# A reloaded weight block moved to dead key storage, and a new hand-written order for a sparse attention and gated feed-forward kernel

## The chip, the cores and the metric

The kernel runs on one core of one Trainium2 chip. The core has five engines that run side by side, each with its own queue of instructions, worked off in order: TensorE (PE, with its weight loads as a row of their own, PEld), VectorE (DVE), ScalarE (ACT), GpSimd (POOL) and SyncE (SP). Semaphores make one engine wait for another or for a transfer. The metric is the device time of the one launch in microseconds.

## What is computed

Block-sparse attention over 4 batches, 8 heads, 768 positions and a head size of 64, then a gated feed-forward layer over the 3072 tokens. The reference, cut to what matters:

```python
scores = scale * np.matmul(q, k.transpose(0, 1, 3, 2))
mask = (np.abs(blk_i - blk_j) <= 1) | first and last block row and column
for qb in range(n_blocks):
    for kb in sampled_blocks[qb]:
        mask[block qb, block kb] = True
attn = softmax(np.where(mask, scores, -1e9))
x = (attn @ v) as tokens x 512
gate = 1.0 / (1.0 + np.exp(-(x @ w_gate)))      # 512 x 1536
return (gate * (x @ w_val)) @ w_out             # 1536 x 512
```

## The kernel before, in words

The work is cut into 12 units, numbered 0 to 11: four batches of three blocks of 256 query rows. Each unit has four pairs of heads, p = 0 to 3. Everything is float16 on the way into TensorE.

For a unit n and a pair p, three steps j make scores (a task `s{n}.{p}.{j}.qk` on PE), each followed by the exponential on ACT (`.exp`, line 597, 128x1024 values). When the three are done, one product with the 0/1 mask on DVE follows (`s{n}.{p}.3.mask`, line 624, 128x3072 float16 values, both operands and the result in SBUF). Then PE multiplies with the values in two halves (`pv{n}.{p}.a` and `.b`), DVE normalizes (`nrm`), and a transposing DMA on SP's queue (`xc`) turns the result.

The feed-forward layer follows in groups g of one or two units. A task `f{g}.{j}` has two halves on PE, then a tanh on ACT (`.th`, line 823) and a gating product on DVE (`.ga`, line 826). The product with `w_out` is done for five pairs of units as a seven-product scheme (`z1` to `z5`: products `A`, `B`, `P3`, `P4`, `P5` on PE; sums of operands `S1` to `S4` on DVE, line 962; results `p1`, `u2`, `c11`, `u3`, `c22`, `c12`, `c21` on DVE, line 1027, or as a plain scaled copy on ACT, line 1101, or DVE, line 1103). Units 0 and 11 go without it (`y0`, and `y11` in the method `y_last`). The scheme needs four differences of blocks of `w_out`; one of them, `T3`, is written over the block `wo[:, 0:HF, UQ:2*UQ]` of `w_out` itself (HF is 6, UQ is 256). So `y_last`, which needs that block once more, gets it by a second load from HBM, the task `ldw0` (line 1086).

Batches 1 to 3 are loaded one batch ahead, for each pair p, by three tasks on GpSimd's queue (line 220): `ldk{b}.{p}`, `ldq{b}.{p}`, `ldv{b}.{p}`, 192 KB each, into `k16`, `q16` and `v16`. For k and q a copy follows into a ring of four buffers `pr` (`kup{b}.{p}`, `qup{b}.{p}`), and a transposing DMA on SP's queue (`kxb`, `qxb`, line 545) into `kT` or `qT`. For v a copy into `vex` follows (`vc{b}.{p}`). These copies are short and any of three engines may make them: POOL (line 279), ACT (line 277) or DVE (line 281). After the copies of batch 3 nothing reads `k16` again.

Nothing in the kernel decides the order while it runs. All 1066 tasks are listed first (`plan.add`), and the string `ORDER` says in which order they are emitted: a number is a task; a letter behind it (A, D, G) chooses another engine than the task's first; `:2` is the PSUM bank (four of them) that a task takes; `@457` makes a load wait until the PE task 457 is done. `j3` is filler work on PE. Each engine gets its tasks in the order in which they stand in this string, and works them off in that order. A load on POOL that waits at its gate holds everything that stands behind it on POOL.

The tasks of which the prediction speaks, by number: 457 is `s5.0.2.qk`, 539 `s6.0.1.qk`, 374 `ldk2.2`, 414 `ldk2.3`, 271 `kup2.0`, 383 `s4.1.0.qk`; 168 and 116 are `ldv1.1` and `ldv1.0`, 220, 181, 257 and 262 `vc1.1`, `vc1.0`, `vc1.2` and `vc1.3`, 365 and 327 the mask products `s3.3.3.mask` and `s3.2.3.mask`, 234 and 228 the gatings `f1.5.ga` and `f1.3.ga`, 300 and 367 `pv3.0.a` and `pv3.2.a`; 245 is `ldq1.3`, 260 and 258 `qup1.3` and `kup1.3`, 261 and 259 their transposes, 328 `s3.3.0.qk`; 556 is `s6.1.1.qk`, 287 `ldv2.0`, 302 `vc2.0`, 560 `s6.1.3.mask`, 562 `pv6.0.a`; 518, 519, 520 and 521 are `z2.c11`, `z2.u3`, `z2.c22` and `z2.P3.a`.

Of the kernel before, what the change touches and what calls it, by code (L numbers as in the profile page):

```python
# [19 lines left out]
B, H, S, D = 4, 8, 768, 64  # L20
# [19 lines left out]
FFN_LAG = 3  # L40
VW = 80
ORDER = """
j3 j3 j3 j3 j3 j3 j3 j3 6 17 14 11A 7:0 18:3 8 15:2 19A 16 9:1 23:0 38:3 39 40:2 24 10 21:0 41 86:1
26:3 87A 82:2 22 27 42:0 46:1 43 47 83 12:3 31:2 13 32 33:0 34 36:3 37 84:2 28:0 62:1 63 85 50:2 51
29 70:0 96@70 20 88:3 44:1 30 71 89 52:2 72:3 90:0 45 73 56:1 91 53 74:3 4@56 0@56 3@56 25 149@56 75
60:2 66:0 80:3 81 57 61 54:1 92:2 48:3 67 111:0 93 112 55 113:1 114 225@113 49 64:3 35 97:2 76:0 65
125@113 98 106:3 77 107 68:1 78:2 69 121:0 79 99:1 122 58:3 100 59 144:2 145 165:1 123:3 124 115
130:0 131 126:2 132 133 147:3 146 166 148 103:0 127 138:1 128 104 134:3 2@103 139 129 109:1 110
1@103 94:0 163:2 135 95 136 179:1 180 164 137 153:0 105 182:1 5@182 154 251:2 252 150:3 183 193:2
151 194 155 167 240:0 241 156:1 152 157 117:2 201 108@240 184:3 191 185 118 187:0 192 158 249:2 202  # L50
169:1 223:3 188 250 140:0 170 224 141 205:2 189:0 171 198@205 206 161G 190 243:3 244 199:0 200 195
172 159:2 258 160A 221:0 173 162 203:3 101:2 186@203 102 245@203 142G 143 238G 222 174 204 218:0 177
196:2 175D 197 259 253 276:3 219 277 207 212:1 282:2 213 214 260A 242 247G 283 209:3 210 211 215:1
261 265:2 216 235 217 266 239 168@265 236 237 273:3 255:1 263:2 274 264 256 119:0 268 120 284:3 269
270 248 285 116@284 328:0 275 329 279 246 229:2 230 231 286 363:1 220G 361:3 362 364 232:0 208@361
325:2 233 326 305:3 226:1 181 234 254@305 300:0 287@305 303:2 306 365 278@303 257G 330@303 227 228
262G 301 304 320 446@303 389:3 449G 390 321 327 322 292:1 380:2 381 293 294 295 331 367:3 410:2 358
178 368 375 432:0 411 280G 370:1 433 376 377 371 296:2 372:0 373 297 267@372 332 366@372 298 333 386
299 383:3 384 288:1 391:0 392 289 316:2 290 302G 435:3 317 382 312:0 437@435 291 412:1 385@412 436
318 681@412 307@412 393 319 323G 313 176 413 314 315 407:3 441:1 442 408 460:2 427 308:0 461 434  # L60
443:1 428 309 444 463:2 399:1 429 438 450:3 310 311 464 335 336 447:0 530:2 281 451 400 445 448
338:3 531 401 402 337 414@530 457:2 324 339 374@457 454 458 341 532:1 533 342 347:2 271G 359A 369
455 272 343 589@532 387G 456 452:1 340 482:0 334 344 348 346 349 453 353:1 459 483 345 539:0 504:3
350 540 430G 505 354 465:0 466 351 484:3 355 378G 395:1 501:0 485 352 480:2 388 467 396 537:3
597@537 481 502 561@537 498 360 397 538 462 398 564G 419:0 503 547:1 548 499 500 558:3 559 420 421
472:1 379 575:2 439 576 422 565:3 473 535:0 566 403:2 536 529 567:3 440 474 534 431 475 404 550:1
542 568 490:3 405 406 394@550 409G 617@550 551 543 544 593:2 491 549 594 492 493 556:1 415:0 553
578:2 557 560 416 579 417 418 423:1 586:3 587 562:2 424 563 425 584:3 585 476:0 426 570 614:1 615
603:3 577 604 571 572 477 468:1 588 581 606:2 478 479 590:3 607 469 591 470 471 598 595:2 596
552@595 599 600 658:0 486:1 605 612:2 696G 554G 633:3 487 632G 659 660@633 613 634 494:0 630:2 495  # L70
488 496 616 489 655:3 497 631 650 506 357 656 592 609 618:1 651 652 676:0 677 507 619 620 356 638:3
580@676 678:0 541@678 639 733:2 679 621 509:1 608@733 640 641 734 747:0 748 742:3 508 510 512D 518:2
582G 583 743 513 511 635:0 727:3 636 569@727 519 514 728 735:0 736 697:3 698 515 516 657 517 626:0
520 740:3 627 730:1 741 628 521 680 694:3 731 629 545G 546 601G 522 695 699:1 674A 700 673 523 755:0
724 555 524:2 725 756 737 767:1 602 768 525 726 622:0 526 753:3 573 574 754 729 661:1 623 624 610
625 646:2 662 663 738:3 750:0 751 647 739 664 648 770:1 744 669:0 649 760:2 771 637@760 527 761 745
762:1 763 670 749 746 671 672 642:2 682:1 643 644 773:3 774 758:0 683 757 759 645 764 848:3 684
665:2 765 752 685 849 686:1 675 666 667 766 769 775:0 668 687 690:3 776 611 688 790:0 653G 654 831:2
691 791 832 777 808 689 811:2 692 693 701 702 772 732 812 778:1 829:3 830 809 850:2 779 851 780 810
782:3 893:2 894 781 704:0 814:1 792:2 793 528 705 703 707D 708 783 815 784 794:2 800:1 795 709 878:2  # L80
# [5 lines left out]
962:0 963 856 864:2 854 926:1 858D 859 921:0 927 922 865 860 920 943:1 945:0 903 944 857 946 861 863  # L86
# [4 lines left out]
1029 1038 1049 1005 1006:0 1031:2 1007 1032 1033 1050 1030 1015:3 1009D 1010 1039:1 1011 1040 1041  # L91
1012 1034 1016 1042 1014 1021:2 1043:1 1008 1017 1022 1018 1023 1025 1044 1026 1019 1045 1013D 1020
1051:2 1052 1046 1053 1054 1056:0 1057 1058 1061:3 1062 1063 1024 1059 1055 1064 1065 1060
# [58 lines left out]
def kernel(  # L152
# [153 lines left out]
    def both(bank):  # L306
        return units_ps[bank.slot]
# [28 lines left out]
    def tiled(out, lhsT, rhs, start, stop):  # L336
        return nc.tensor.matmul(out, lhsT, rhs, start=start, stop=stop, skip_group_check=True).ins  # L337
# [441 lines left out]
    class Ffn:  # L779
# [168 lines left out]
        def z(self, mate):  # L948
# [129 lines left out]

            stored[0] = [plan.add(key + "st0", [(SP, 0.45)], store(0, b, u), [c11, c12], dma=("O", 0))]
            stored[1] = [plan.add(key + "st1", [(SP, 0.45)], store(1, b2, u2), [c21, c22], dma=("O", 0))]  # L1080
            if self.z_ == last_z:
                back.append(
                    plan.add(
                        "ldw0",
                        [(DMA, 0.72)],
                        lambda eng: nc.gpsimd.dma_start(  # L1086
                            wo[:, 0:HF, UQ : 2 * UQ],
                            moe_w_out.rearrange("(f p) m -> p f m", p=128)[:, 0:HF, UQ : 2 * UQ],
                        ),
                        [pb, t3],  # L1090
                        dma=("L", 0.393),
                    )
                )
# [86 lines left out]
    def later(b):  # L1180
# [155 lines left out]
```

## Time and profile before

| | us |
|---|---|
| median of 3 runs | 284.26 |
| lowest and highest of them | 282.92, 290.8 |
| the profiled execution's own time | 282.64 |
| its span, first to last instruction | 280.9 |
| PE busy within the span | 270.7 |
| DVE, ACT, POOL busy within the span | 210.6, 187.7, 76.9 |

Times within the profile count from the first instruction. A row of a view of groups gives line, engine, operation, what is written and read, how often, the sum of busy time and the mean of one in ns, then the engine's idle time ahead of it and what ended that. A row of the timeline gives start and duration in us, and in brackets the engine's idle time ahead and what ended it. The table by stretches gives busy time of each engine, the granted clock of TensorE as a share, the share of the DMA engines and GB/s.

### The profile page before, as it was taken

To read this page: it belongs to the slowest core of one execution; us is meant where nothing else is said; L and a number is where in the kernel's file an instruction comes from. 1 tells how busy PE (TensorE), PEld (TensorE's weight loads), DVE (VectorE), ACT (ScalarE), POOL (GpSimd) and SP (SyncE) were. 2 spreads that over 40 slices of the span, in tenths; PEclk is the share of its full clock that TensorE was granted. 3 is DMA by queue.
4 is the path that set the end of the run, shared out by engine and by line. 5 is a ranking of instruction groups with operands and counts; after the bars stand their busy time and mean duration, and the time that the engine had idled before them with its cause. 6 is when DMAs were issued, how large, how long until landed. Compare 5 with 4: busy or idle time off the path is not lost.

```text
span 280.9 us, 11919 instructions
## 1 busy us (share of the span) xinstructions
PE 270.7 (96%) x5459; PEld 208.6 (74%) x5459; DVE 210.6 (75%) x282; ACT 187.7 (67%) x231; POOL 76.9 (27%) x98
## 2 busy tenths in 40 slices
PE   6899999999899989999999999999999999999995
PEld 2677886777789869889787666678656876759983
DVE  4568685879998998689978877977669868537371
ACT  2699888789799768889788676875765753323100
POOL 8966432345756552222451012000000000000010
PEclk9799999999999999999999999999999999999999
DMA  7999999969879897854899338200330401040063
GB/s 152 181 195 196 200 203 156 130 106 144 119 138 131 124 182 66 105 74 109 140 120 122 94 56 119 97 2 5 126 44 5 57 5 77 2 116 0 2 133 149
DMA packets 55434, 29.36 MB, mean 105 GB/s; under 512 B 32308, under 2 KB 53708, under 8 KB 55384
## 3 DMA queue, kind: packets, MB, share of 16 engines
q0 software_dynamic: 22384, 14.33, 37.6%
q1 hardware_dynamic: 32512, 13.98, 27.5%
q8 instruction: 42, 0.69, 1.0%
q10 hardware_dynamic: 488, 0.30, 0.3%
q14 instruction: 8, 0.07, 0.1%
HBM read 29.25 MB, written 6.29 MB: 127 GB/s over the span
## 4 chain that ended last, share of the span: by engine, by line
PE 71%; DMA 14%; POOL 6%; DVE 4%; ACT 2%; issue 1%; ACTq 0%; POOLq 0%
PE m L337 71%; DMA wv<-in_moe_w_val_dram 7%; DMA wo<-in_moe_w_out_dram 3%; DMA q<-in_q_dram 2%; DMA kT<-pr 2%; DVE P L624 2%; POOL k L220 1%; POOL q L220 1%; ACT P L597 1%; DVE ht L826 1%; POOL v L220 1%; POOL wg L230 1%; DVE sums L962 1%; ACT th L823 1%; POOL wv L230 1%
## 5 line engine op out<-in xcount | busy, mean ns | idle before, releaser
L597 ACT ACTIVATE P<-m 128x1024 f16<-128x1024 f32 x144 | 142.2, 1024 | 31.9 <-PE m L337 30.2
L337 PE MATMUL m<-xTs,wg 64*128 64x256 f16 (+2 forms) x768 | 137.8, 310 | 0.3 <-DVE ysb L1103 0.2
L337 PE MATMUL m<-xTs,wv 64*128 64x256 f16 (+2 forms) x768 | 137.9, 310 | 0.0
L337 PEld LDWEIGHTS <-wg 64*128 64x128 f16 (+1 forms) x768 | 70.4, 94 | 16.1 <-issue 1.7
L624 DVE TENSOR_TENSOR P<-P,mask 128x3072 f16<-128x3072 f16 x44 | 80.9, 1845 | 1.2 <-ACT P L597 1.2
L337 PEld LDWEIGHTS <-wv 64*128 64x128 f16 (+1 forms) x768 | 70.2, 94 | 14.9 <-issue 0.4
L823 ACT ACTIVATE th<-m 128x512 f32<-128x512 f32 x72 | 42.8, 599 | 45.0 <-PE m L337 44.6
L826 DVE SCALAR_TENSOR_TENSOR ht<-th,m 128x512 f16<-128x512 f32 x72 | 48.7, 683 | 30.5 <-ACT th L823 30.1
L337 PE MATMUL m<-qT,kT 64*128 64x256 f16 x576 | 53.8, 271 | 1.4 <-DMA kT<-pr 0.9
L337 PEld LDWEIGHTS <-P 64*128 64x128 f16 (+1 forms) x2112 | 44.9, 94 | 8.2 <-issue 1.7
L337 PE MATMUL m<-vex,P 64*128 64x65 f16 (+1 forms) x2112 | 48.3, 190 | 1.2 <-DVE P L624 0.8
L337 PE MATMUL m<-wo,ht 64*128 64x256 f16 (+3 forms) x444 | 41.6, 284 | 0.1
L337 PEld LDWEIGHTS <-ht 64*128 64x128 f16 (+1 forms) x564 | 35.3, 94 | 6.2 <-DVE wsum L962 0.5
L337 PEld LDWEIGHTS <-kT 64*128 64x128 f16 x576 | 26.5, 94 | 11.0 <-issue 2.6
L1086 POOL DMA_DIRECT2D wo<-in_moe_w_out_dram x1 | 0.8, 840 | 97.2 <-PE m L337 97.2
L337 PEld LDWEIGHTS <-sums 64*128 64x128 f16 x360 | 23.3, 94 | 2.9 <-issue 0.4
L1027 DVE SCALAR_TENSOR_TENSOR ysb<-m,ysb 128x512 f32<-128x512 f32 x25 | 17.2, 689 | 7.3 <-PE m L337 4.9
L220 POOL DMA_DIRECT2D q<-in_q_dram x19 | 13.9, 729 | 19.6 <-PE m L337 12.3
L650 DVE TENSOR_TENSOR x16s<-m,rz 128x512 f16<-128x512 f32 (+1 forms) x28 | 17.2, 615 | 1.0
L220 POOL DMA_DIRECT2D k<-in_k_dram x15 | 10.9, 724 | 23.2 <-PE m L337 22.0
L279 POOL COPY pr<-k 128x768 f16<-128x768 f16 x9 | 10.6, 1188 | 19.6 <-DMA kT<-pr 11.7
L337 PE MATMUL m<-early,sums 64*128 64x256 f16 x120 | 14.7, 269 | 0.1
(63 smaller groups left out, 167.3 us busy)
## 6 DMA issues: line engine op xcount, KB each, us to landing
out_dram<-ysb SPq DMA_DIRECT2D x10, 512.0 KB, 2.9
v<-in_v_dram POOLq DMA_DIRECT2D x16, 192.0 KB, 4.9
k<-in_k_dram POOLq DMA_DIRECT2D x15, 192.0 KB, 5.0
q<-in_q_dram POOLq DMA_DIRECT2D x12, 192.0 KB, 4.9
wg<-in_moe_w_gate_dram POOLq DMA_DIRECT2D x6, 256.0 KB, 8.2
wv<-in_moe_w_val_dram POOLq DMA_DIRECT2D x6, 256.0 KB, 9.1
wo<-in_moe_w_out_dram POOLq DMA_DIRECT2D x6, 256.0 KB, 9.7
out_dram<-ysb SPq DMA_DIRECT2D x3, 256.0 KB, 3.3
```

The source lines that it names most:

```text
L220: return nc.gpsimd.dma_start(dst[:, h0:h1, t0:t1, :], src[b, h0:h1].rearrange("h (p t) d -> p h t d", t=NT)[:, :, t0:t1, :],)
L230: nc.gpsimd.dma_start(dst[:, :, f0:f1], src.rearrange("(c p) f -> p c f", p=128)[:, :, f0:f1])
L279: nc.gpsimd.tensor_copy(dst, src)
L337: return nc.tensor.matmul(out, lhsT, rhs, start=start, stop=stop, skip_group_check=True).ins
L597: nc.scalar.activation(self.pt.rearrange("a h i n -> a h (i n)"), both(self.bank), AF.Exp, bias=0.0, scale=SCALE)
L624: nc.vector.tensor_tensor(pt, pt, m.unsqueeze(1).broadcast_to([128, 2, NT * UQ]), op=ALU.mult)
L650: nc.vector.tensor_tensor(self.x16, acc[:, :, :, 0:D], rz.broadcast_to([128, w, 2, D]), op=ALU.mult)
L823: nc.scalar.activation(th, both(bank)[:, 0, :], AF.Tanh, bias=0.0, scale=0.5)
L826: nc.vector.scalar_tensor_tensor(self.ht[:, tiles[0] : tiles[-1] + 1, :], in0=th.rearrange("a (f n) -> a f n", n=self.w), scalar=1.0, in1= ...
L962: nc.vector.tensor_tensor(dst, x, y_, op=op)
L1027: nc.vector.scalar_tensor_tensor(dst, in0=src(), scalar=0.5, in1=add, op0=ALU.mult, op1=ALU.add)
L1086: lambda eng: nc.gpsimd.dma_start(wo[:, 0:HF, UQ : 2 * UQ], moe_w_out.rearrange("(f p) m -> p f m", p=128)[:, 0:HF, UQ : 2 * UQ],),
```

## The change

Three things are changed. First, `ldw0` no longer writes the block back into `wo`, but into the first half of `k16`, seen as `wo12`; so it need no longer wait for the last use of `T3`, only for the batch-3 copies out of `k16`. It is listed after the last unit (and gets number 1003 for 1026; tasks 1003 to 1025 of before are one higher), and stands on POOL behind `vc3.3`, with no gate. Second, `y_last` reads the first six slices of that block from `wo12`. Where its output is 512 wide, the product of each of these slices becomes two products of 256 columns, since the two halves of the weights now lie in two tiles. Third, the whole string `ORDER` is another one, found by a search in which a copy on GpSimd and a product of two SBUF operands on VectorE can't run at the same time.

```diff
-            if self.z_ == last_z:
-                back.append(
-                    plan.add(
-                        "ldw0",
-                        [(DMA, 0.72)],
-                        lambda eng: nc.gpsimd.dma_start(
-                            wo[:, 0:HF, UQ : 2 * UQ],
...
-                        [pb, t3],
...
                         for f in range(f0, f0 + 4):
-                            tiled(
-                                both(bank)[:, 0, 0 : c1 - c0],
-                                self.ht[:, f, i * UQ + s * 128 : i * UQ + (s + 1) * 128],
-                                wo[:, f, c0:c1],
-                                f == 0,
-                                f == NF - 1,
-                            )
+                            parts = [(c0, c1)] if f >= HF or c1 - c0 == UQ else [(0, UQ), (UQ, DM)]
+                            for a, b in parts:
+                                tiled(
+                                    both(bank)[:, 0, a - c0 : b - c0],
+                                    self.ht[:, f, i * UQ + s * 128 : i * UQ + (s + 1) * 128],
+                                    wo12[:, f, :] if f < HF and a == UQ else wo[:, f, a:b],
+                                    f == 0 and a == c0,
+                                    f == NF - 1,
+                                )
...
+    wo12 = k16.rearrange("a h t d -> a (h t d)")[:, 0 : HF * UQ].rearrange("a (f m) -> a f m", m=UQ)
+
+    def reload():
+        back.append(
+            plan.add(
+                "ldw0",
+                [(DMA, 0.72)],
+                lambda eng: nc.gpsimd.dma_start(
+                    wo12, moe_w_out.rearrange("(f p) m -> p f m", p=128)[:, 0:HF, UQ : 2 * UQ]
+                ),
+                [x for p in range(NP) for x in copies["k", B - 1, p]],
+                dma=("L", 0.393),
+            )
+        )
...
     do(turned, Pair.xt)
+    reload()
     while parts:
         part_of(len(units))
```

The two orders share most of their shape: of the 464 PE tasks the kinds (scores of a unit, value product of a unit, feed-forward half of a group) match in sequence for 339. In the new one POOL makes 29 copies for 24. To POOL go `kup1.1`, `qup1.1`, `qup1.3`, `vc1.0`, `qup2.1`, `qup2.3`, `qup3.2` and `qup3.3`; from POOL to DVE go `vc1.1` and `vc3.0`, to ACT `kup2.3`; `vc3.1` goes from DVE to ACT. POOL's queue at the four places that the prediction treats, the gate behind the `@`:

```
before  ... ldv1.1@s3.0.1.qk ldv1.0@s3.1.2.qk vc1.1 ldv1.2@s3.3.1.qk ldv1.3@s3.2.1.qk ldv2.0@s3.2.1.qk
            ldq2.0@s3.2.0.qk vc1.2 ldq2.1@s3.2.0.qk vc1.3 ...
after   ... ldv1.1@s3.0.0.qk ldv1.0@s3.0.0.qk vc1.2 ldv1.3@s3.3.2.qk vc1.0 ldk2.1@s3.2.2.qk
            ldv2.2@s3.2.0.qk vc1.3 ...
before  ... kup2.1 ldk2.3@s5.3.1.qk ldk2.2@s5.0.2.qk kup2.0 ldv3.1@s5.3.2.qk qup2.2 ...
after   ... ldk2.0@s4.0.2.qk ldq2.0@s4.0.0.qk kup2.1 ldk2.3@s4.2.2.qk kup2.0 ldq2.1@s4.1.0.qk ...
before  ... ldk1.2@s2.1.1.qk ldq1.3@s2.1.1.qk kup1.0 ...          (qup1.3 on ACT)
after   ... ldv1.2@s2.2.1.qk ldq1.3@s2.2.1.qk kup1.0 qup1.3 ...   (SP: qxb1.3, then kxb1.3)
after   ... kup3.0 ldv2.0@s6.1.1.qk ldk3.2@s6.1.1.qk ldq3.3@s7.0.0.qk vc2.2 vc2.3 vc2.0 ...
```

More of the change, by code (lines that the diff above doesn't have):

```diff
@@ L42 @@
 ORDER = """
[L43 to L75, printed above, removed]
@@ L86 @@
[L86 removed]
[4 rows of a table removed]
[L91 to L93 removed]
+j3 j3 j3 j3 j3 j3 j3 j3 14A 6 7:0 8 15:3 11 17A 18:2 9:1 16 23:0 24A 19 40:3 41 12:2 21:0 10 13A 22
+38:1 26:3 82:2 39 50:0 51 27 86:1 2@50 83 36:3 37 87 31:2 33:0 42:1 32 34 28:2 43 84:0 29 70:3 85
@@ new lines @@
+88:2 225@70 89 60:1 71 125@60 61 80:0 81 52:2 72:3 53 20 73 4@52 0@52 56:0 57 46:1 47 44:3 35 66:2
+67 25 74:0 149@66 90:1 45 92:3 93 75 62:0 63 91 111:2 112 3@111 30 1@111 54:1 55 64:3 5@111 108@111
+97:0 65 113:1 114 191G 192 98 48:3 49 76:2 106:0 68:3 77 58:1 96@106 99:2 107 69 78:3 59 144:1 145
+100 121:2 130:0 131 122 186@121 115 132 201G 79 202 123:1 124 165:2 133 166 126:3 147:0 146 103:1
+104 127 128 138:2 134:1 139 109:2 129 148 110 163:3 164 94:0 135 179:2 153:3 136 180 137 182:2
+198@182 95 154 251:0 105 150:1 155 252 183 193:0 167 240:3 194 156:2 117:0 151 152 157 158 187:1 241
@@ new lines @@
+118 249:2 169:3 159:0 250 188 221:1 222 160 161G 184:2 189:0 190 170 185 203:0 140:1 171 141 199:1
+200 205:2 172 204 223:1 208@223 245@223 258 173 195 101:0 206 142G 243:2 224 102 143 162 244 174
+218:1 177 196:0 276:2 219 197 175D 209:3 277 282:0 260G 212:2 210 242 253 207 283 261 213 214 215:0
+265:2 211 238G 235 284:3 216 217 236 266 285 255:0 259 273:2 247G 274 248 239 256 237 119:1 120 268
+263:3 269 168@263 116@263 328:1 270 229:2 361:0 264 275 257G 329 279 363:3 230 231 286 254@363 362
@@ new lines @@
+220 364 232:1 233 234 305:2 181G 325:0 307@325 226:3 326 306 300:1 227 365 303:0 304 301 320 246
+394@303 389:2 390 228 321 327 292:3 380:0 381 262G 293 322 367:2 294 267@380 410:0 368 358 370:1 375
+295 331 411 278@370 371 296:3 176 332 432:0 433 323G 376 414@432 372:1 373 297 298 377 333 299 288:0
+391:2 383:1 392 289 312:3 290 271G 272 330@383 435:2 382 291 384 436 313 314 316:1 412:0 413 393
+407:2 317 408 315 318 319 441:0 308:3 280G 442 427 460:1 309 434 461 310 281 386 428 429 463:0 464
@@ new lines @@
+311 335 336 437@463 399:1 569@463 446@463 443:2 444 400 324 450:0 447:3 448 530:2 451 531 338:0 359G
+366@530 385@530 445 457:2 580@457 401 339 374@457 454 458 337 402 347:2 455 532:1 178 341 342 430A
+343 431 533 456 360 482:3 483 452:1 340 334 453 344 348 346 345 387G 349 539:3 353:1 540 504:0 350
+354 465:3 505 459 466 351 378G 379 355 484:0 485 352 395:1 501:3 502 480:2 467 537:0 396 481 498 388
+538 558:3 397 419:0 398 499 573 547:1 559 541@547 500 462 503 420 439G 438 548 421 422 545G 534
@@ new lines @@
+565:3 566 472:2 575:1 576 473 474 403:3 567:0 568 369 535:1 404 405 536 475 556:0 287@556 557 542
+406 490:2 597@556 357 550:3 593:0 549 543 544 551 491 594 440 660@593 529 409G 492 493 415:3 449G
+578:1 586:0 302G 416 587 560 417 418 579 423:2 562:0 424 425 584:1 585 563 553 426 570 476:3 552@584
+577 582G 603:2 604 614:1 615 356 571 572 477 478 583 468:2 606:0 607 590:1 588 469 591 598 479 470
+595:0 596 471 599 600 658:3 659 486:2 633:0 612:1 487 605 494:3 613 616 630:1 634 495 631 650 488
+489 496 497 506 676:0 655:2 589@655 581 677 574 651 652 637@655 609 508 618:3 546 507 656 638:0
@@ new lines @@
+678:2 679 747:1 619 620 639 608@747 674G 509:2 621 748 680 640 742:3 733:1 641 743 510 518:3 635:0
+734 554G 727:1 512D 513 519 636 514 728 657 697:0 561@697 617@697 555 699:1 515 610G 698 511 517 700
+516 626:0 740:1 627 741 520 521 694:2 628 735:1 522 695 724 729 629 736 523 755:0 730:1 524:3 725
+673 601G 525 756 622:0 731 750:1 592A 726 751 602 762:2 526 738:3 653G 763 623 737 739 767:1 744 624
+625 661:2 745 746 632G 768 770:0 662 646:1 771 663 760:3 761 642:0 664 753:2 754 749 647 681@753
@@ new lines @@
+696G 648 669:3 643 644 649 775:2 776 670 682:1 757 654 758:2 683 759 645 671 684 672 764 773:0 685
+774 675 814:3 732 815 765 766 690:1 665:0 769 564 831:2 611 832 811:3 812 666 691 692 777 686:2 752
+772 790:3 667 668 693 687 791 527 808 688 689 701 703 829:0 830 702 778:1 782:2 809 810 891:0 892
+779 780 781 783 704:0 794:3 784 848:1 795 849 785 705 800:2 792:3 793 884:1 528 885 833 801 707D 708
[5 rows of a table added]
+980:1 982:2 981 923 983 856 864:0 858D 859 926:1 921:2 857 865 927 860 922 962:1 963 903 945:2 861
@@ L94 @@
+984 862D 946 863 866 929:1 933:2 870:3 920 934 935 936 930 931 932 871 872 867 947:2 943:1 967:3 868
[6 rows of a table added]
 """
@@ L1144, in y_last @@
                         lag=0.0 if f0 < 8 else None,
-                        ops=8,
+                        ops=8 + 2 * (c1 - c0 == DM) * max(0, min(4, HF - f0)),
                         wide=True,
```

10 lines of the change are left out of this document (removed), and 20 rows, old and new, of the table ORDER.

## The prediction

> **What bounds the kernel now.** I read the page first, then the busy time by stretches, the chain of waits, and the timeline around each place where PE stood idle.
>
> ```profile
> span 280.9 us, 11919 instructions
> ...
> PE 270.7 (96%) x5459; PEld 208.6 (74%) x5459; DVE 210.6 (75%) x282; ACT 187.7 (67%) x231; POOL 76.9 (27%) x98
> ```
>
> TensorE is the bound: it is busy for 270.7 of 280.9 us. The change leaves PE's arithmetic as it is, so all that an order can win is PE's idle time, 10.2 us. The table by stretches says where that lies.
>
> ```profile
> 0.00:20.00 20.00, 16.81 (x301) 10.18 (x303) 11.86 (x32) 12.00 (x14) 16.83 (x27) 0.91 1.16 175
> 20.00:160.00 140.00, 136.38 (x3022) 112.35 (x3018) 117.92 (x149) 117.34 (x141) 56.81 (x69) 1.00 0.94 132
> 160.00:272.40 112.40, 112.14 (x2111) 82.68 (x2107) 78.45 (x99) 57.99 (x77) 3.26 (x3) 1.00 0.25 54
> 272.40:281.00 8.60, 5.38 (x36) 3.43 (x36) 2.40 (x4) 0.38 (x1) 0.00 (x0) 1.00 0.39 154
> ```
>
> The second number of a row is PE's busy time. Idle are 3.2 us in the first 20 us (the first loads), 3.6 from 20 to 160, 0.3 up to 272.4, and at the end 3.1 us of the last copy and store behind PE's last matmul (280.9 less 272.4, less 5.38). What an order can reach is thus mainly the 3.6 us between 20 and 160, or 1.3% of the span. A gain of 2% would take 5.7 us, which is more than that; it would need the start shortened as well.
>
> **The change part by part.** All is summed against the profiled execution's own 282.64 us (span 280.9, 1.7 around it). That is 0.6% under the median of the runs shown, 284.26, and next to their lowest, 282.92.
>
> *The reload.* Before, it is issued late and PE meets its landing:
>
> ```profile
> L337 PEld LDWEIGHTS <-ht 128*128 128x128 f16 x36 | 3.4, 98 | 2.0 <-DMA wo<-in_moe_w_out_dram 0.3
> 272.39 5.38 PE L337 MATMUL m<-wo,ht 128*128 128x512 f16 x36
> ```
>
> Nothing stands behind it on POOL. What the wait for it costs is at most the weight loads' 0.3 us. The new load waits for the batch-3 copies and for `vc3.3` ahead of it, both around 170 us (`kup3.3`, below, runs at 168.8), and has 100 us to land. I take 0.2 of the 0.3 us; zero is the least. Six products of 512 columns become twelve of 256: the 36 matmuls of 5.38 us hold 48 pieces of 256 columns (12 are 512 wide), 0.112 us a piece, and columns stay the same. Six more weight loads of 98 ns fit behind pieces of 112 ns; if nothing hid them, they would cost 0.6. I take 0. The order of the last two evacuations is swapped, so that DVE, not ACT, makes the last one, of the same size: left out.
>
> *The k copy at 96 us.* The chain of waits, then PE:
>
> ```profile
> 95.67 0.71 POOL k L220
> 96.38 0.84 POOL pr L279
> ...
> 97.25 5.69 DMA kT<-pr
> ```
> ```profile
> 102.98 0.61 PE L337 MATMUL m<-qT,kT 64*128 64x256 f16 x8 [0.88 <-DMA kT<-pr]
> ```
>
> `kup2.0` stood on POOL behind `ldk2.2`, whose gate opens just before 95.67; load issue, copy and transpose take 7.3 us, and PE waits 0.88 us for `s6.0.1.qk`. In the new order `kup2.0` stands ahead of `ldk2.2` and behind `ldk2.3`, gated on `s4.2.2.qk`, one unit earlier: more than 15 us of PE work are to spare. All of the 0.88 goes; I take 0.9. `ldk2.2` itself keeps its gate, and its block is used some 9 us later than `kup2.0`'s was; with 0.71 for one more load ahead, 5.3 to land (as worked out below), two copies of 0.84 and 5.69, it needs 13.4 us from the gate and has 15.9 us by the order. That is next, 2.5 us off.
>
> *The mask product at 72 us.* POOL, DVE, PE:
>
> ```profile
> 71.79 0.83 POOL L279 COPY vex<-v 128x768 f16<-128x768 f16 x1
> ...
> 73.27 2.25 POOL L279 COPY vex<-v 128x768 f16<-128x768 f16 x1
> ```
> ```profile
> 68.12 0.35 DVE L281 COPY vex<-v 128x768 f16<-128x768 f16 x1
> 68.39 0.68 DVE L826 SCALAR_TENSOR_TENSOR ht<-th,m 128x512 f16<-128x512 f32 x1
> 68.99 1.75 DVE L624 TENSOR_TENSOR P<-P,mask 128x3072 f16<-128x3072 f16 x1
> 70.74 0.69 DVE L826 SCALAR_TENSOR_TENSOR ht<-th,m 128x512 f16<-128x512 f32 x1
> 71.86 2.98 DVE L624 TENSOR_TENSOR P<-P,mask 128x3072 f16<-128x3072 f16 x1 [0.43 <-ACT P L597]
> ```
> ```profile
> 70.01 0.54 PE L337 MATMUL m<-vex,P 64*128 64x65 f16 x24
> 74.90 0.54 PE L337 MATMUL m<-vex,P 64*128 64x65 f16 x24 [0.79 <-DVE P L624]
> ```
>
> A product that meets no copy takes 1.75 us; this one began with a copy running, and took 2.98, and the copy at 73.27 took 2.25 instead of 0.83, to just behind the product's end. Whoever is second waits for the whole of the other. PE paid 0.79 us for it at `pv3.2.a`. The new order has other copies here, and its clashes must be counted. Its gates for `ldv1.1` and `ldv1.0` open where the second of these loads was issued before:
>
> ```profile
> 60.00 0.71 POOL L220 DMA_DIRECT2D v<-in_v_dram  x1
> 62.97 0.72 POOL L220 DMA_DIRECT2D v<-in_v_dram  x1 [2.26 <-PE m L337]
> 65.39 0.99 POOL L279 COPY vex<-v 128x768 f16<-128x768 f16 x1 [1.70 <-DMA v<-in_v_dram]
> ```
>
> A load issued at 60.00 let its copy start at 65.39, so 5.3 us to land. After: `ldv1.1` at 62.97, landed at 68.3, its copy now on DVE (0.35) to 68.65, `f1.5.ga` (0.68) to 69.3, then `s3.3.3.mask`. `ldv1.0` at 63.69, landed by 69.0, its copy now on POOL from 69.0 to 69.85, 0.3 us ahead of the product, in time for `pv3.0.a` at 70.01: cost 0. The product waits to 69.85 and ends at 71.6, `f1.3.ga` at 72.3; `vc1.3`, behind a load that shares the gate of the one ahead of the copy at 71.79, starts at about 71.8 too and ends at 72.6, so `s3.2.3.mask` runs from 72.6 to 74.35. PE wants it at 74.11 (74.90 less 0.79): a wait of 0.3 stays. I take a gain of 0.5, between 0.8 and the loss of the rival below.
>
> *The seven-product scheme at 150 us.* DVE and PE:
>
> ```profile
> 150.23 1.42 DVE L1027 SCALAR_TENSOR_TENSOR ysb<-m,ysb 128x512 f32<-128x512 f32 x2 [1.16 <-ACT ysb L1101]
> 151.70 0.50 PE L337 MATMUL m<-wo,sums 64*128 64x256 f16 x6 [0.26 <-DVE ysb L1027]
> ```
>
> `z2.u3` on DVE waited for `z2.c11`, on ACT. The new order emits `u3` ahead of `c11`: the 0.26 goes.
>
> *What is added.* `kxb1.3`, needed by `s3.3.0.qk` at 62.89, stands behind `qxb1.3` on SP, where before it stood ahead and only `qxb1.3` was late. `ldq1.3` is gated 1.1 us of PE work earlier than before (half a `y0` task, 0.87, and a score task, 0.22, by the costs in the plan), when it was issued at 51.49 and let a copy start at 57.22. So it lands at about 56.1; a POOL copy of 0.84 ends at 57.0, SP takes 1.22 for the first transpose, and the second lands 4.5 (the median of kT) after 58.2, at 62.7.
>
> ```profile
> 51.49 0.72 POOL L220 DMA_DIRECT2D q<-in_q_dram  x1
> 57.22 0.83 ACT L277 COPY pr<-q 128x768 f16<-128x768 f16 x1 [1.82 <-DMA q<-in_q_dram]
> 58.08 1.22 SPq L545 DMA_TRANSPOSE qT<-pr  x1
> 62.89 0.38 PE L337 MATMUL m<-qT,kT 64*128 64x256 f16 x4
> kT<-pr SPq DMA_TRANSPOSE x12, 4.5
> ```
>
> In time by 0.2; with the transpose at 5.69, as above, 1.0 late. I take 0.2. `vc2.0` is new just ahead of `pv6.0.a` (122.75). Its load opens where this one did:
>
> ```profile
> 117.23 0.71 POOL L220 DMA_DIRECT2D v<-in_v_dram  x1 [1.31 <-PE m L337]
> 120.88 0.97 POOL L279 COPY vex<-v 128x768 f16<-128x768 f16 x1 [2.94 <-DMA v<-in_v_dram]
> 122.75 0.53 PE L337 MATMUL m<-vex,P 64*128 64x65 f16 x24
> ```
>
> It lands after 3.6 us, at 120.9. Ahead of its copy stand two loads, the second gated on `s7.0.0.qk`, and two copies of 0.83, from about 119.9 on, so `vc2.0` runs from 121.6 to 122.4. I take 0.1; if `s6.1.3.mask` gets in first, it is a product later, up to 1.5. Eight copies go to POOL and three leave it; DVE has four fewer (4 times 0.35), ACT one fewer. Neither bounds the kernel, so 0. The start has the same first loads: 0, with half a microsecond either way, since copies there change between DVE and ACT.
>
> Sum: 282.64 - 0.2 - 0.9 - 0.5 - 0.26 + 0.2 + 0.1 = 281.1 us. The ends: nothing added, all removed, start shorter by 0.5: 282.64 - 0.3 - 0.9 - 0.8 - 0.3 - 0.5 = 279.8, and 279.0 if small waits near by go too. Both clashes lost and the transpose late: 281.1 + 1.9 + 1.4 + 0.8 = 285.2.
>
> **A rule weighed.** Before, a load issued at 165.22 while a product ran still let its copy start 3.5 us later:
>
> ```profile
> 165.22 0.71 POOL L220 DMA_DIRECT2D k<-in_k_dram  x1 [13.24 <-PE m L337]
> 168.76 1.70 POOL L279 COPY pr<-k 128x768 f16<-128x768 f16 x1 [2.82 <-DMA k<-in_k_dram]
> 164.22 1.75 DVE L624 TENSOR_TENSOR P<-P,mask 128x3072 f16<-128x3072 f16 x1
> ```
>
> The Trainium skill's page "SBUF — State Buffer", in "SBUF: two separate sides", says that a DMA issued by GpSimd can't get its descriptors written while VectorE runs an operation that holds the port which both share. By that rule `ldv1.0`, issued in the new order under a product, would land late, which is rival C; the row shows no such delay.
>
> **The rivals.** *A, slower: a copy loses its port at `pv3.0.a`.* If `ldv1.0` lands later than 5.6 us after its issue (69.3 less 63.69), the product goes first, to 71.05; the copy ends at 71.9, and PE waits 1.9 us, of which the 0.3 at `pv3.2.a` is got back or not: 282.7 to 283.0, say 282.9. For it: 5.3 us was seen, only 0.3 less. Against it: DVE waits for `ldv1.1` ahead, so both slip together. *B, the freed waits are taken up by the next:* the orders are alike, and PE is fed by many short leads; with half of the 1.7 us lost again, 282.0, with all, 282.6. For it: from 160 to 272.4 us PE is idle for 0.3 us alone, so a task that is late there by less than its cover shows in no view. Against: the two large waits had slack of several us behind them. *C, the rule above:* `ldv1.0` one product (1.75) later: 282.85. *D, the order does more than I count*, also at the start: 279.5.
>
> **How the numbers follow.** The forecast's own case (280.3 to 282.0) 0.48, A 0.17, B 0.18, C 0.03, D 0.08, and 0.06 for something worse that I do not see, 285 and more. Predicted is 281.1. The range of 279.1 to 284.8 leaves out part of D and most of the last. A measurement of this kernel tells about 2% from no change: faster than 277.0 would take more than all reachable idle time, and only the far part of D goes there, 0.06; slower than 288.3 needs more than the three clashes at once, 0.05, most of the last case; within, 0.89.
>
> **What would show it.** Right: no idle time of PE ended by kT near 103 us; the largest product of line 624 between 42 and 80 us under 2.4 us; no idle time of the weight loads from the reload, and the reload issued near 170 us; DVE's line 1027 with less idle time ended by ACT. Wrong: idle time of PE ended by a POOL copy of vex near 70 or 122 us (A), or the same PE busy time with more short waits (B), or a start whose first 20 us hold more than 3.7 us of idle time.

## The result, and the profile after

| kernel | median us (lowest to highest) | ratio to the kernel before, 95% interval |
|---|---|---|
| changed | 284.87 (283.23 to 289.08) | 1.0061 (1.0035 to 1.0087) |
| the same again, in another session | 284.34 (283.59 to 285.83) | 1.0050 (1.0025 to 1.0075) |

Forecast were 281.1 us, 1.5 less than the profiled execution's 282.64. The changed kernel is slower, by 0.6% or 1.7 us; that is less than 2%, and more than its interval. The ratios leave out slow executions, and the first profile of the changed kernel is of one of these, so that of the second session, its own time 284.34, stands for it. Its page begins:

```profile
span 282.6 us, 11928 instructions
...
PE 269.5 (95%) x5465; PEld 215.5 (76%) x5465; DVE 214.1 (76%) x277; ACT 188.6 (67%) x231; POOL 81.3 (29%) x103
```

The span has grown by 1.7 us, as the times have. PE is not busier; DVE is, by 3.5 us, although it got four copies less. The timeline of PE shows where it stood idle. These are all its rows with 0.2 us or more of it ahead of them, between 55 and 160 us:

```profile
59.66 0.40 PE L337 MATMUL m<-qT,kT 64*128 64x256 f16 x4 [0.39 <-DVE ht L826]
74.64 0.54 PE L337 MATMUL m<-vex,P 64*128 64x65 f16 x24 [0.44 <-DVE P L624]
81.89 0.27 PE L337 MATMUL m<-xTs,wg 64*128 64x256 f16 x1 [0.79 <-DVE ht L826]
94.51 0.28 PE L337 MATMUL m<-early,sums 64*128 64x256 f16 x1 [0.76 <-DVE sums L962]
118.65 0.27 PE L337 MATMUL m<-xTs,wg 64*128 64x256 f16 x1 [0.58 <-DVE ht L826]
130.26 0.40 PE L337 MATMUL m<-qT,kT 64*128 64x256 f16 x4 [0.22 <-DVE x16s L650]
155.94 0.61 PE L337 MATMUL m<-qT,kT 64*128 64x256 f16 x8 [0.25 <-DVE ht L826]
```

The wait of 0.88 us for `kT` near 103 us is gone, and that at `pv3.2.a` fell from 0.79 to 0.44. In their place stand waits that the prediction does not have: `f2.4.a` (81.89), `z1.A` (94.51), `f4.4.a` (118.65), `s7.1.0.qk` (130.26). All of them end with VectorE. What made it late is on DVE and POOL, here between 75 and 95 us:

```profile
75.93 0.95 DVE L962 TENSOR_TENSOR wsum<-wo 128x1536 f16<-128x1536 f16 x1
76.92 1.76 DVE L962 TENSOR_TENSOR early<-wo,wsum 128x1536 f16<-128x1536 f16 x1
...
79.44 1.79 DVE L962 TENSOR_TENSOR wo<-wo 128x1536 f16<-128x1536 f16 x1
81.16 0.68 DVE L826 SCALAR_TENSOR_TENSOR ht<-th,m 128x512 f16<-128x512 f32 x1
...
91.47 1.49 DVE L962 TENSOR_TENSOR sums<-ht 128x1536 f16<-128x1536 f16 x1
93.00 1.46 DVE L962 TENSOR_TENSOR sums<-sums,ht 128x1536 f16<-128x1536 f16 x1
```
```profile
77.02 0.84 POOL L279 COPY pr<-k 128x768 f16<-128x768 f16 x1
...
79.58 0.84 POOL L279 COPY pr<-k 128x768 f16<-128x768 f16 x1
...
92.52 1.11 POOL L279 COPY pr<-q 128x768 f16<-128x768 f16 x1
```

`zt1` to `zt3` are the sums that make three of the scheme's differences of `w_out`; in the rows they write `wsum`, `early` and `wo`. `zt1` met no copy and took 0.95 us. `zt2`, of the same size, has its row from 76.92, met `kup2.1` and took 1.76; `zt3` met `kup2.0`, 1.79; `z1.S1` and `z1.S2` met `qup2.1`, 1.49 and 1.46. In the kernel before, no copy on POOL lay beside these four, and DVE had:

```profile
78.11 0.95 DVE L962 TENSOR_TENSOR early<-wo,wsum 128x1536 f16<-128x1536 f16 x1
78.97 0.95 DVE L962 TENSOR_TENSOR wo<-wo 128x1536 f16<-128x1536 f16 x1
...
90.71 0.96 DVE L962 TENSOR_TENSOR sums<-ht 128x1536 f16<-128x1536 f16 x1
91.70 0.96 DVE L962 TENSOR_TENSOR sums<-sums,ht 128x1536 f16<-128x1536 f16 x1
```

In the changed kernel, from 76 to 82 us, DVE had nothing to spare, so the 1.65 us that `zt2` and `zt3` lost made `f2.2.ga` (81.16) late, and PE waited 0.79 us behind it. Between 112 and 118 us it is the same with a mask product and a copy on DVE (DVE, then POOL), which met `qup2.3` and `kup3.0`:

```profile
112.04 2.80 DVE L624 TENSOR_TENSOR P<-P,mask 128x3072 f16<-128x3072 f16 x1
...
117.03 0.98 DVE L281 COPY vex<-v 128x768 f16<-128x768 f16 x1
```
```profile
112.38 0.83 POOL L279 COPY pr<-q 128x768 f16<-128x768 f16 x1
115.84 1.96 POOL L279 COPY pr<-k 128x768 f16<-128x768 f16 x1 [2.62 <-issue]
```

This leads to **theory D**: the 1.7 us are lost where a copy on GpSimd meets an instruction on VectorE that works on SBUF alone, at places where the prediction counted nothing. Rivals: **S**, the late transpose that the first profile showed (below); **N**, the new order gives its waits up elsewhere, whatever the copies do (rival B of the prediction).

### The profile page after: what moved, and what is told of

Same layout as the page of the kernel before. It is cut to its first block, busy times and chain, and to the rows that moved or that the text cites. A ratio compares the mean times of both kernels' runs of the same rounds, so it can differ in the third digit from the quotient of the medians.

```text
span 287.3 us, 11928 instructions
## 1 busy us (share of the span) xinstructions
PE 273.4 (95%) x5465; PEld 215.6 (75%) x5465; DVE 212.8 (74%) x277; ACT 188.9 (66%) x231; POOL 82.5 (29%) x103
## 4 chain that ended last, share of the span: by engine, by line
PE 71%; DVE 15%; DMA 7%; POOL 3%; issue 2%; ACT 1%; DVEq 0%; SPq 0%; ACTq 0%
PE m L337 71%; DVE P L624 6%; DMA q<-in_q_dram 3%; DVE ht L826 2%; DMA v<-in_v_dram 2%; DMA xTs<-x16s 2%; DVE sums L962 2%; DVE x16s L650 1%; ACT th L823 1%; POOL k L220 1%; POOL q L220 1%; POOL v L220 1%; DVE wo L962 1%; DVE ysb L1027 0%; ACT P L597 0%
## 5 line engine op out<-in xcount | busy, mean ns | idle before, releaser
L337 PE MATMUL m<-xTs,wg 64*128 64x256 f16 (+2 forms) x768 | 140.3, 314 | 4.7 <-DMA xTs<-x16s 3.5
L337 PE MATMUL m<-xTs,wv 64*128 64x256 f16 (+2 forms) x768 | 140.2, 314 | 0.0
L337 PEld LDWEIGHTS <-wg 64*128 64x128 f16 (+1 forms) x768 | 71.7, 96 | 19.4 <-DMA xTs<-x16s 3.8
L624 DVE TENSOR_TENSOR P<-P,mask 128x3072 f16<-128x3072 f16 x44 | 82.2, 1871 | 1.4 <-ACT P L597 1.3
L337 PEld LDWEIGHTS <-wv 64*128 64x128 f16 (+1 forms) x768 | 71.4, 96 | 14.9 <-issue 1.4
L337 PE MATMUL m<-wo,ht 64*128 64x256 f16 (+2 forms) x438 | 41.1, 283 | 0.0
L337 PEld LDWEIGHTS <-ht 64*128 64x128 f16 (+1 forms) x570 | 36.9, 94 | 4.6 <-issue 0.4
L337 PEld LDWEIGHTS <-kT 64*128 64x128 f16 x576 | 27.8, 95 | 9.9 <-issue 3.7
L220 POOL DMA_DIRECT2D v<-in_v_dram x16 | 11.6, 730 | 41.2 <-PE m L337 41.2
L279 POOL COPY pr<-q 128x768 f16<-128x768 f16 x12 | 12.3, 1026 | 9.5 <-DMA q<-in_q_dram 6.5
```

The source lines that it names most:

```text
L220: return nc.gpsimd.dma_start(dst[:, h0:h1, t0:t1, :], src[b, h0:h1].rearrange("h (p t) d -> p h t d", t=NT)[:, :, t0:t1, :],)
L279: nc.gpsimd.tensor_copy(dst, src)
L624: nc.vector.tensor_tensor(pt, pt, m.unsqueeze(1).broadcast_to([128, 2, NT * UQ]), op=ALU.mult)
```

## Experiments

Fifteen kernels ran, in four groups; the kernels of a group ran on the same chip, and each ratio is to the kernel before in the same group. In the diffs, numbers are tasks of `ORDER`, and `...` marks what is left out; a task that is put in at a new place is taken out at its old one, which the diffs do not always show. *Lag* in the expectations is the start of a PE task less the PE work that stands ahead of it.

**Is it the late transpose?** In the first profile of the changed kernel PE and the clock show this (timeline of PE, table by stretches):

```profile
115.33 0.39 PE L337 MATMUL m<-xTs,wg 64*128 64x256 f16 x1 [3.53 <-DMA xTs<-x16s]
```
```profile
115.00:120.00 5.00, 4.67 (x45) 3.23 (x47) 2.35 (x2) 1.62 (x2) 2.13 (x1) 0.50 0.60 134
```

`xc4.1` stood on SP behind the transposes of a k block that landed late. The changed kernel ran again unchanged, and with `xc4.3` (462) and `xc4.1` (438) ahead of `kxb2.2` (379); a third kernel has the order before and the reload alone, behind `kup3.3` (653).

```diff
-378G 379
+378G 462 438 379
```

> The changed kernel as it is, once more, for a second profile. Theory S (SP's queue): two transposes of the attention result, xc4.3 and xc4.1, stand on SP behind two transposes for k and q that wait for the load ldk2.2; in the changed kernel's profile this let PE idle for 3.5 us at f4.1 (115.33). If the wait is of the order, this profile has it again, between 1 and 4 us, since it hangs on when ldk2.2 lands. Theory C (a clock dip that happened once): the idle time at that place is under 0.5 us, and the loss sits elsewhere. Time about 284.9.

> The changed kernel with xc4.3 and xc4.1 moved on SP's queue ahead of kxb2.2 and qxb2.2. Theory S: the wait at f4.1 goes whole, and nothing behind it takes its place at once, since kxb2.2 is used 9 us of PE work later: 281.5 to 283 us, ratio to before 0.992 to 0.998. Theory D (DVE): the loss is made of clashes of the GpSimd copies with the sums of the seven-product scheme between 75 and 95 us, some 2 us; then the time stays within 0.5 us of the changed kernel, about 284.5.

```diff
-653G 654
+653G 1003 654
```

> The order of before, with the reload into the k block alone, issued behind the last k copy, and the split products. Prediction: 0.0 to 0.3 us faster than before, ratio 0.999 to 1.000. Rival: the twelve narrower products and six more weight loads cost up to 0.6 us, ratio up to 1.002.

Measured: 1.0050 (1.0025 to 1.0075), 1.0051 (1.0032 to 1.0070), 1.0015 (0.9980 to 1.0049). The long wait was in no profile of the first two, and the loss was there all the same: S falls as its cause. (The wait itself came again in two later profiles of kernels without that move, below.) The third ratio agrees with no change and tells nothing of 0.3 us; its profile shows a wait of its own on PE:

```profile
179.51 0.39 PE L337 MATMUL m<-qT,kT 64*128 64x256 f16 x4 [1.53 <-DMA kT<-pr]
```

In the order before, the reload goes out at 171.77 on POOL, 0.4 us ahead of the last k transpose at 172.20 on SP, and PE waits 1.53 us for that. In the changed order `kup3.3` runs some 17 us earlier, and PE has no wait there.

**Clear the meetings.** Copies were moved off the places where they meet: at 75 to 95 us `kup2.1` (323) to DVE and `qup2.1` (359) to ACT; at 110 to 130 us `qup2.3` (439) and `qup3.1` (582) to DVE's idle time and `vc2.1` (369) behind `f3.2.ga` (406); then all of these, with `kup3.2` (601) and `kup3.3` (653) on DVE.

```diff
-433 323G 376
+433 376
...
-434 461
+434 323D 461
...
-338:0 359G 366@530 385@530 445 457:2 580@457 401 339
+338:0 366@530 385@530 445 457:2 401 359A 580@457 339
```

> The changed kernel with two copies taken off GpSimd: kup2.1 to VectorE behind s4.2.3.mask, qup2.1 to ACT behind f3.1.th, so that neither meets zt2, zt3, z1.S1 or z1.S2. Theory D (the time is lost where GpSimd's copies and VectorE's scheme sums meet): zt2, zt3, S1 and S2 last 0.95 us each again, PE's 0.79 us of idle time at f2.4.a goes and so does most of the 0.85 at z1.A; 1.0 to 1.7 us less than the changed kernel, ratio to the kernel before 0.999 to 1.002. Theory N (the order gives its waits up elsewhere, whatever the copies do): sums shorter, but the time stays within 0.4 us of the changed kernel, ratio 1.004 to 1.006.

```diff
-573 547:1
+573 439D 547:1
...
-568 369 535:1
+568 535:1
...
-406 490:2
+406 369 490:2
...
-418 579
+418 582D 579
```

> The changed kernel with other copies moved: qup2.3 and qup3.1 from GpSimd to VectorE where it stands idle, and vc2.1 behind f3.2.ga. Theory D: s5.2.3.mask lasts 1.75 us instead of 2.8, vc2.1 0.35 instead of 1.0, s6.2.3.mask 1.75 instead of 2.4, and the waits of PE at s6.2.1.qk, f4.4.a and s7.1.0.qk (0.45, 0.74 and 0.39 us of lag) go: 1.0 to 1.5 us less than the changed kernel, ratio 1.000 to 1.003. Theory N: within 0.4 us of the changed kernel, 1.004 to 1.006.

```diff
-592A 726
+592A 601D 653D 726
```

> Both of these together, and kup3.2 and kup3.3 from GpSimd to VectorE ahead of nrm7.3, so that s8.0.3.mask near 152 us meets no copy. Theory D: the gains add up, 2.3 to 3.5 us less than the changed kernel, 0.5 to 1.7 us less than the kernel before, ratio 0.994 to 0.998. Theory N: 1.003 to 1.006.

Measured: 1.0019 (0.9983 to 1.0054), 0.9964 (0.9931 to 0.9998), 0.9941 (0.9892 to 0.9990). The first interval holds both theories. The second kernel gained more than D had said (1.000 to 1.003); the three waits that its profile no longer has make up 1.05 us of it. With the second region cleared, PE's rows at 118, 130 and 156 us are gone and those of the first are left as they were:

```profile
81.59 0.27 PE L337 MATMUL m<-xTs,wg 64*128 64x256 f16 x1 [0.79 <-DVE ht L826]
94.34 0.28 PE L337 MATMUL m<-early,sums 64*128 64x256 f16 x1 [0.75 <-DVE sums L962]
```

That speaks for D and against N: a wait that was cleared did not come up elsewhere. The profiles of the first and the third had the long wait near 115 us again, 3.04 and 2.44 us, so the first region was cleared again later.

**The predicted steps alone, and added copies.** Two kernels have the order before with `kup2.0` (271) ahead of `kup2.1` (323), its transpose (272) ahead of `kxb2.1` (324), and `z2.u3` (517) ahead of `z2.c11` (516). In the first of them I put `z2.u3` ahead of the mask product 657 as well, which the product then had to wait for.

```diff
-319 323G
+319 271G 323G
...
-457:2 324
+457:2 272 324
...
-515 516 657 517 626:0
+515 517 516 657 626:0
```

> The kernel before, with two steps of the change alone: kup2.0 ahead of kup2.1 on GpSimd and its transpose ahead of kxb2.1 on SP, and z2.u3 emitted ahead of z2.c11. If the two terms of the prediction are right (0.9 us for the transpose's wait at s6.0.1.qk, 0.26 for z2.u3), 0.8 to 1.2 us less than the kernel before, ratio 0.996 to 0.997. If freed waits are taken up by the next (rival B), 0 to 0.5 us less, ratio 0.998 to 1.000.

```diff
-515 516 657 517 626:0
+515 657 517 516 626:0
```

> The kernel before with kup2.0 ahead of kup2.1 and its transpose ahead of kxb2.1, and z2.u3 between s7.2.3.mask and z2.c11 (in the run before it stood ahead of that mask as well). If the prediction's two terms are right: no wait at s6.0.1.qk (0.88 us), none of 0.26 at z2.P3.a, 0.8 to 1.2 us less than the kernel before, ratio 0.996 to 0.997. Rival B: 0.998 to 1.000.

Measured: 0.9971 (0.9927 to 1.0016) and 0.9975 (0.9925 to 1.0025): undecided between the two theories. In the profile of the second the waits at `s6.0.1.qk` and `z2.P3.a` are gone, and PE has two new ones that nothing in the profile ends, 1.12 us at 98.52 and 1.20 us at 110.89. Moving `kup2.0` need not have caused the first of them: at the same products it is 1.05 us (99.41) in the kernel with `z2.u3` alone, below, where `kup2.0` was not moved.

The other kernels of that group: the changed order with all copies cleared, `qup2.1` on POOL ahead of `ldq2.3` (437), and the `xc4` transposes first; the same with the start of the order before (its diff is left out); and the order before with three copies more.

```diff
-336 437@463
+336 359G 437@463
```

> The changed kernel with all moves of the run that cleared all clashes, but qup2.1 stays on GpSimd, ahead of ldq2.3 (about 86 us, where no scheme sum runs), and xc4.3 and xc4.1 stand ahead of kxb2.2 on SP. Theory D: 2.5 to 4 us less than the changed kernel, span 278 to 280 us, ratio to the kernel before 0.990 to 0.995; no idle time of PE over 0.5 us between 75 and 135 us, also none at f4.1.a. Theory N: 1.003 to 1.006.

> The candidate of this group with the first tasks (up to vc0.2, about 20 us) in the order of the kernel before; three loads are gated a few tasks later for it. If the start of the changed kernel costs the 0.3 to 0.9 us of lag that its traces show at 25 us against the kernel before, this one is 0.3 to 0.9 us faster than the candidate; if that lag is only swing of the first loads, the two agree within 0.3 us.

```diff
-389:3 449G
+389:3 1066 1067 1068 449G
...
+    spare = sums.rearrange("a i f m -> a (i f m)")[:, 0:768]
+    for _ in range(3):
+        plan.add("spare", [(DMA, 0.83)], lambda eng: nc.gpsimd.tensor_copy(spare, wg[:, 0, 0:768]))
```

> The kernel before, its order kept, with three more GpSimd copies of 128x768 f16 that nobody reads, put ahead of vc2.3, where GpSimd stood idle for 3.9 us (76.5 to 80.45 us). Theory D: zt2 waits behind them (2 to 2.6 us instead of 0.95), f2.2.ga comes 1.0 to 1.6 us later and PE loses 0.7 to 1.5 us near 80 us; ratio 1.002 to 1.005. Theory N, and any in which GpSimd's copies on idle GpSimd time cost nothing: 0.999 to 1.001, no new idle time of PE at 80 us.

The first gave 0.9956 (0.9909 to 1.0002), 281.88 us, and one wait of 0.51 us was left between 75 and 135 us, at `s4.3.2.qk`. The second is a miss: 291.86 us, because PE waited 6.55 us at 53.59 for a load of the output weights, which stood behind another gate once the two orders were joined; it says nothing of the start. The third gave 1.0012 (0.9970 to 1.0053), and DVE, POOL and PE show what was expected of D, if smaller, and at `zt1` and `zt3` instead of `zt2`:

```profile
76.57 2.00 DVE L962 TENSOR_TENSOR wsum<-wo 128x1536 f16<-128x1536 f16 x1
...
80.20 1.58 DVE L962 TENSOR_TENSOR wo<-wo 128x1536 f16<-128x1536 f16 x1
```
```profile
76.91 4.05 POOL L1307 COPY sums<-wg 128x768 f16<-128x768 f16 x3
```
```profile
82.42 0.27 PE L337 MATMUL m<-xTs,wg 64*128 64x256 f16 x1 [0.49 <-DVE ht L826]
```

Copies that nobody reads, on time that POOL had idle, lengthened `zt1` and `zt3` by 1.68 us together, and gave PE a wait of 0.49 us at the feed-forward half where the changed kernel waits. In the time of the runs so little can't be seen: the interval holds both theories.

**What was left open.** Four more kernels: the changed order with all cleared, now with `kup2.1` ahead of `f2.5.ga` (319) and `vc1.3` (262) on DVE behind `s3.2.3.mask` (327); the first region alone; the reload alone, gated on `s10.0.2.qk` (878); `z2.u3` alone, edited as above.

```diff
-327 292:3
+327 262D 292:3
...
-318 319
+318 323D 319
```

> The candidate of the last group with two more copies moved to idle time of VectorE: kup2.1 ahead of f2.5.ga instead of behind s4.2.3.mask (it met qup2.1 there, 0.99 us instead of 0.35), and vc1.3 from GpSimd to VectorE behind s3.2.3.mask. Theory D: the 0.5 us wait at s4.3.2.qk and that at pv3.2.a go, 0.4 to 0.9 us less than the candidate, span 278.8 to 279.5 us, ratio to the kernel before 0.989 to 0.994. Theory N: 1.003 to 1.006.

> The changed kernel with only the meetings of 75 to 95 us cleared (kup2.1 on VectorE ahead of f2.5.ga, qup2.1 still on GpSimd but ahead of ldq2.3, so before z1.S1) and xc4.3 and xc4.1 ahead of kxb2.2, which alone changed nothing. Theory D: no wait of PE at f2.4.a (0.79 us) and none at z1.A (0.76); those at f4.4.a and s7.1.0.qk stay; 1.0 to 1.7 us less than the changed kernel, ratio 0.999 to 1.002. Theory N: 1.004 to 1.006.

```diff
-878:2 785
+878:2 1003@878 785
```

> The order of the kernel before with the reload into the dead keys alone, gated on s10.0.2.qk (about 188 us) so that it does not meet the transposes of kxb3.3. If the 1.5 us wait at s9.3.2.qk of the earlier run came from the reload's transfer, it is gone, and the time is that of the kernel before less 0 to 0.3 us, ratio 0.999 to 1.000; if it came from something else in the changed code, it stays, ratio 1.004 to 1.006.

> The kernel before with z2.u3 emitted ahead of z2.c11 (still behind s7.2.3.mask) and nothing else. If the term of the prediction is right, PE's 0.26 us at z2.P3.a goes and the time falls by 0.2 to 0.3, ratio 0.999; rival B: another wait takes its place, 1.000. If the idle time of 1.1 to 1.4 us in the middle of the group z1.B.a, seen in the two kernels where kup2.0 was moved, shows here as well, moving kup2.0 did not cause it.

Measured: 0.9932 (0.9899 to 0.9964), 280.28 us; 0.9991 (0.9958 to 1.0024), 282.32 us; the last two gave no ratio, so only their profiles count, one of each. With the first region alone cleared, PE waits at neither `f2.4.a` nor `z1.A`, and the two waits of the second region are still there, the first of them smaller:

```profile
116.03 0.27 PE L337 MATMUL m<-xTs,wg 64*128 64x256 f16 x1 [0.32 <-DVE ht L826]
127.64 0.39 PE L337 MATMUL m<-qT,kT 64*128 64x256 f16 x4 [0.22 <-DVE x16s L650]
```

With all cleared, the table by stretches shows what PE gained against the changed kernel. First the rows of the changed kernel, then those of the cleared one:

```profile
80.00:110.00 30.00, 28.36 (x696) 25.69 (x692) 26.82 (x27) 24.75 (x29) 9.70 (x13) 1.00 1.00 134
110.00:160.00 50.00, 48.78 (x1205) 44.36 (x1202) 45.66 (x50) 39.82 (x48) 18.12 (x22) 1.00 0.68 111
```
```profile
80.00:110.00 30.00, 29.81 (x744) 27.37 (x740) 26.34 (x32) 26.13 (x31) 11.17 (x14) 1.00 1.04 150
110.00:160.00 50.00, 50.00 (x1254) 43.96 (x1250) 44.09 (x53) 41.67 (x51) 13.30 (x18) 1.00 0.69 102
```

PE is busy for 2.7 us more in these 80 us. This kernel beats both: 0.4 to 1.0% under the kernel before. With the reload gated, and issued at 198.47, PE has no wait at `s9.3.2.qk`; that fits its transfer as the cause of the 1.53 us, with one profile on each side. `z2.u3` alone stays undecided.

## Why the prediction was wrong

The step that failed is in "What is added": *Eight copies go to POOL and three leave it; [...] Neither bounds the kernel, so 0.* The prediction had seen that a copy on GpSimd and a product on VectorE hold each other up, and counted it with mask products, at the places that it went through. It did not count the mask products elsewhere, nor the other instructions of VectorE that read and write SBUF, the scheme's sums (line 962) and DVE's own copies, and it took DVE's 75% of busy time for slack. In two stretches of the changed kernel DVE had next to none, and the first was nearly as full in the kernel before (DVE's busy time is the second number; the last row is of the kernel before):

```profile
62.90:81.90 19.00, 18.25 (x21) 1.00 0.93 127
112.00:121.00 9.00, 8.98 (x9) 1.00 0.60 93
```
```profile
62.00:82.00 20.00, 18.66 (x21) 1.00 1.05 142
```

The mask products show how much more they met: before, changed, and with all cleared, from the view of groups (44 at 1.75 us are 77.0):

```profile
L624 DVE TENSOR_TENSOR P<-P,mask 128x3072 f16<-128x3072 f16 x44 | 80.9, 1845 | 1.2 <-ACT P L597 1.2
```
```profile
L624 DVE TENSOR_TENSOR P<-P,mask 128x3072 f16<-128x3072 f16 x44 | 83.5, 1903 | 1.7 <-ACT P L597 1.7
```
```profile
L624 DVE TENSOR_TENSOR P<-P,mask 128x3072 f16<-128x3072 f16 x44 | 79.3, 1805 | 1.4 <-ACT P L597 1.3
```

That is 3.9, 6.5 and 2.3 us over 77.0. The sums of line 962 took 1.8 us more in the changed kernel than before. Why an order whose search kept such pairs apart meets so often is not shown here. Term by term:

| term | forecast us | in the changed kernel |
|---|---|---|
| reload's wait at the end | -0.2 | the reload is issued at 170.9 and hidden; from `y11.0.0.0` to the end of the span 8.51 us in both kernels, so about 0 |
| `kT` at `s6.0.1.qk` | -0.9 | -0.88: right in the profile; as a saving of time it was not settled alone |
| mask product at 72 us | -0.5 | -0.35; the product lasts 2.63 us, not under 2.4: `vc1.3` got in first |
| `z2.u3` | -0.26 | its wait is gone: right in the profile |
| `kxb1.3` behind `qxb1.3` | +0.2 | no wait at `s3.3.0.qk`: 0 |
| `vc2.0` ahead of `pv6.0.a` | +0.1 | no wait: 0 |
| all else | 0 | +0.79, +0.76, +0.58, +0.22; +0.25 at `s8.3.2.qk` (155.94), behind a product that met `kup3.2` and `kup3.3`; +0.39 at `s3.0.1.qk` (59.66), behind one that met `qup1.3`; this one stays with all cleared |

From 20 us on, PE's rows with 0.2 us or more of idle time ahead of them add up to 2.93 us before and to 4.07 in the changed kernel. That is 1.1 of the 1.7; where the rest lies stays open. It may be the start, where the changed kernel's profile has the sign that the prediction named, 4.8 us of idle time in the first 20 us. But that swings: it was 3.2 and 5.0 us in two profiles of the order before, 4.8 and 3.6 in two of the changed one, and the one kernel that was to settle it missed. Rival A did not come: PE has no wait at `pv3.0.a`. Rival C is seen nowhere: `ldv1.0`, the second of two loads issued from 63.23 on, with a product running from 64.19, let its copy start at 68.38, within the 5.6 us that it had. Of rival B the sign is there, more short waits at the same busy time of PE, but not its cause: in the kernel with all cleared, no row of PE behind 60 us has 0.2 us of idle time ahead of it. Whether the gain of the two predicted steps alone is taken up elsewhere stays open. The chance of 0.06 for "something worse that I do not see" is the case that came, if less bad than the 285 us given with it. Two of the four removed waits came as forecast, one in part and the reload's not; the cost of the added copies, put at 0, outweighed them. Two readings were off without weight: the load of 60.00 took 5.4 us to land, not 5.3, and the copy at 73.27 ended 0.7 us behind the product, which is not just behind it.

That `zt2` waits for all of the copy (1.76 is 0.95 and 0.81) agrees with the Trainium skill, page "SBUF — State Buffer", section "SBUF: two separate sides": the port pair that VectorE and GpSimd share is an exclusive lock for the whole instruction, and an operation with two SBUF inputs contends with a GpSimd instruction that reads SBUF. The page gives the pair to the one that starts first; here the row of `zt2` begins 0.1 us ahead of the copy's, so the rows' starts do not tell who got it. The prediction cited the page for the load and could have taken the lock from it for the sums.

## What to carry to other kernels

A copy that is moved to an idle GpSimd is not free: list every VectorE instruction that works on SBUF alone, sums and copies as well as products, and lay GpSimd's new copies against each in time; one meeting cost VectorE 0.5 to 1.1 us in the changed kernel. Then ask whether VectorE has slack in that stretch, not over the whole kernel: 76% busy overall was 96% for 19 us. The cheapest place for such a copy was a gap of VectorE itself, 0.35 us for 0.83 on GpSimd, and no meeting.

## What was not expected of the hardware

Two copies that stand back to back on GpSimd can both go ahead of a product that waits. In the changed kernel (DVE, POOL):

```profile
152.48 2.81 DVE L624 TENSOR_TENSOR P<-P,mask 128x3072 f16<-128x3072 f16 x1
```
```profile
152.07 1.60 POOL L279 COPY pr<-k 128x768 f16<-128x768 f16 x2
```

The product came 0.4 us behind the start of the first copy and took 1.06 us over its 1.75, so it waited for the second copy as well. It is no rule: in the kernel with the second region cleared the same product came 0.2 us behind the start of the first copy, took 0.54 us over, and it was the second copy that waited (DVE, POOL):

```profile
150.99 2.29 DVE L624 TENSOR_TENSOR P<-P,mask 128x3072 f16<-128x3072 f16 x1
```
```profile
150.83 3.14 POOL L279 COPY pr<-k 128x768 f16<-128x768 f16 x2
```

Gatings, which read PSUM, kept their 0.68 us beside a copy, as at 68.65 in the changed kernel beside the copy of 68.38.

The wait for `kT` that the change takes away is not steady. In the kernel with `z2.u3` alone, so in the order before, PE and POOL had:

```profile
110.30 1.03 PE L337 MATMUL m<-qT,kT 64*128 64x256 f16 x8 [7.33 <-DMA kT<-pr]
```
```profile
100.58 0.82 POOL L279 COPY pr<-k 128x768 f16<-128x768 f16 x1 [8.62 <-DMA k<-in_k_dram]
```
```profile
110.00:115.00 5.00, 4.70 (x46) 3.33 (x48) 0.69 (x1) 2.58 (x3) 0.83 (x1) 0.50 0.58 119
```

The copy behind that load (`ldk2.0`, issued at 91.22) started 9.4 us after its issue; in the profile of the kernel before it was 5.9 us. All that stood behind it on POOL and SP moved with it, and TensorE's granted clock was 0.50 in the 5 us after the idle time, as it was behind the 3.53 us above. Behind the 3.04 us near 115 us it stayed at 1.00. Why that load is late in some executions stays open, as do the idle times by "issue" in the middle of a group.
